# f32 matmuls as pairs of 64-column tiles on TensorE, in a kernel that mixes f32 and bf16 matmuls

## The chip, the cores and the metric

One core of a Trainium2 chip. The time is device microseconds of one execution. Repeated executions of one kernel on one core scatter here: those of the kernel before lie up to 1.3% below and 2.4% above their median. So beside the times this text uses the lengths of stages read from the profiles, which repeat far better. A stage length comes from one profile of each kernel. Each run also has the mean granted clock of TensorE (1.0 is full speed). A run is marked slow when it is more than 1.5% above the fastest of its kernel; on one core that only means the upper part of the scatter.

## The reference

Linear attention on sketched features, then a Fourier mix with a small MLP. Cut to what matters (batch 4, 4 heads, 1088 positions, head size 32, sketch 8):

```python
def phi(x):                                  # 64 features from two projections of 8
    a, b = S1 @ x, S2 @ x                    # per position
    return outer(a, b).reshape(64)
kv  = sum_s phi(k)[s] (x) v[s]               # 64 x 32 per head ("kv sums")
z   = sum_s phi(k)[s]
out = (phi(q) @ kv) / (phi(q) @ z + 1e-6)    # "numerators" and denominators
# then, per batch: real part of the 2-D FFT, residual, normalization, MLP with ReLU
```

## The kernel before

All work is in a fixed order of steps (a timetable of some 1,100), each on one engine: PE (TensorE, the matmuls), DVE (VectorE), ACT (ScalarE) or POOL (GpSimd). The four batches overlap: attention of batch b+1 runs beside the Fourier mix and MLP of batch b. Attention matmuls have f32 operands, those of the mix bf16. Three kinds of f32 matmul concern us; each uses the full 128x128 array:

```python
# k projections: 9 chunks of 128 positions; the moving operand is 64 columns, twice
PE.matmul(_v(bt(bks[c // 4]), 0, 128, 128 * (c % 4), [[1, 128]]),
          kT(s)[:, 128 * c : 128 * c + 128], _v(sblk, 0, 128, 0, [[0, 2], [1, 64]]),
          start=True, stop=True, skip_group_check=True)
# ... cut ...
# kv sums: 9 chunks x 2 pairs of heads; only the two 64x64 diagonal blocks are read later
rhs = _v(vx(s), 0, 128, 32 * c + 1280 * p, [[320, 4], [1, 32]])
PE.matmul(bt(bkv)[:, 128 * p : 128 * p + 128], _v(kp(s, c), 0, n, 128 * p, [[1, 128]]), rhs,
          start=(seen[0] + seen[1] == 0), stop=(seen[p] == 8), skip_group_check=True)
# ... cut: kvz copies of the sums, by ACT and DVE ...
# numerators: 9 chunks x 2 pairs of heads, 66 columns
PE.matmul(bt(bk)[:, o : o + 66], lh, kvz(s, p, i & 1)[:, :], start=True, stop=True,
          skip_group_check=True)
```

The q projections are f32 too, and already run as eight 32x64 tiles at a time. The bf16 matmuls use the full array. In the profile, tile names tell the groups apart: `sblk,kT` are k projections, `vx,kp` kv sums, `kvz,qp` numerators, `tab,fo` and `tab,xb` the first Fourier stage.

## Time and profile before

| | before |
|---|---|
| median of 3 runs | 107.97 us (106.48 to 109.22) |
| span of the profiled run, mean clock | 106.3 us, 0.969 |
| PE, DVE, ACT busy | 84%, 75%, 47% |
| f32 steps as above (all four batches) | 36 + 72 + 72 = 180 |

From the page of the kernel before: the span, the busy strips (40 slices of 2.66 us; tenths), and lines of two f32 groups on PE (matmul) and PEld (weight load). Columns of a group: total busy us, mean ns of one; then idle time before it.

```profile
span 106.3 us, 2601 instructions
...
PE   5985989999799959999977999999996979998000
...
PEclk9999999999999999999999999999999999999755
DMA  2999999999950090000000000203000212223341
...
L591 PE MATMUL bank<-kvz,qp 128*128 128x66 f32 x144 | 21.8, 263 | 1.1 <-ACT kvz L271 1.1
L591 PEld LDWEIGHTS bank<-kvz,qp 128*128 128x128 f32 x144 | 20.6, 191 | 2.8 <-ACT kvz L271 1.3
L504 PE MATMUL bank<-vx,kp 128*128 128x128 f32 x144 | 19.7, 277 | 1.1 <-DMA vx<-in_v_dram 1.1
```

DMA is full until about 30 us; PE is nearly full from there. Each f32 step has two records (x144 for 72 steps): two passes. Records overlap, so a mean of 263 ns is not the cost of one; the starts are. In the timeline of weight loads, two in a row take 0.30 us though one alone takes 0.19: they start 112 ns apart, whether 66 or 128 columns stream. A step costs 222 ns.

The existing tiled matmuls show that a change of tiling is not free. The weight loads of the kernel before, around a block of q projections:

```profile
22.43 0.30 PEld L591 LDWEIGHTS bank<-kvz,qp 128*128 128x128 f32 x2
22.80 0.23 PEld L543 LDWEIGHTS bank<-qT,eb 32*64 32x64 f32 x16
23.84 0.30 PEld L591 LDWEIGHTS bank<-kvz,qp 128*128 128x128 f32 x2 [0.81 <-ACT ab L271]
```

The last full-array matmul before that block started at 22.595 us and the first tiled load at 22.798, 203 ns later, with no wait that the profile shows; without a change of tiling the load behind a full-array matmul starts 1 to 3 ns after it (633 of 737 in this trace). The recorded texts call this extra time a drain.

The chain of waits (start, length):

```profile
38.36 0.19 ACT kvz L271
38.60 0.66 PE bank L591 x4
...
45.00 0.17 PE bank L591 x2
45.17 0.14 PE bank L646
45.33 0.41 ACT zt L271
...
78.60 0.18 DVE den L596
```

**A** is the start of the first numerator after the kvz copies of batch 1 (38.60 us), **B** the end of the twelfth matmul of the first Fourier stage (45.59), **C** the end of the last numerator matmul (78.49), which releases `den`; **D** the end of the span. Up to A the chain is DMA, then POOL and DVE; from A to B it is PE.

### The profile page before, as it was taken

The numbers are of one execution on the slowest core, as the hardware profiler recorded it, in microseconds if no ns is written. First come the engines' busy times: TensorE is split into PE (matmuls) and PEld (weight loads), VectorE is DVE, ScalarE is ACT, GpSimd is POOL, SyncE is SP. The second block draws the span as 40 slices with busy tenths as digits, with TensorE's granted clock in tenths as the row PEclk, the third lists the DMA queues.
The fourth block names the chain that finished last, engine by engine and source line by source line (L and its number), as shares of the span: only waits on it lengthen the run. The fifth ranks groups of instructions, "written<-read, shape, count | busy, mean of one in ns | idle before, by whom it ended". The sixth has DMA issues, their size and how long they took to land.

```text
span 106.3 us, 2601 instructions
## 1 busy us (share of the span) xinstructions
PE 89.4 (84%) x940; PEld 72.3 (68%) x943; DVE 80.2 (75%) x266; ACT 50.4 (47%) x140; POOL 42.0 (39%) x87
## 2 busy tenths in 40 slices
PE   5985989999799959999977999999996979998000
PEld 3672379969399949997743898739895957756000
DVE  1538969685888846999575999789999799998300
ACT  4011520417101030025579757868866979996000
POOL 8813832099119991419300100321939730500000
PEclk9999999999999999999999999999999999999755
DMA  2999999999950090000000000203000212223341
GB/s 77 291 361 268 261 317 250 301 357 188 253 132 10 7 236 11 0 0 0 9 0 0 0 0 24 81 0 99 3 6 0 72 26 70 60 71 82 102 119 48
DMA packets 9620, 11.14 MB, mean 105 GB/s; under 512 B 1032, under 2 KB 8200, under 8 KB 9608
## 3 DMA queue, kind: packets, MB, share of 16 engines
q1 hardware_dynamic: 8920, 10.70, 37.6%
q10 hardware_dynamic: 688, 0.28, 1.0%
q8 instruction: 7, 0.11, 0.5%
q14 instruction: 5, 0.04, 0.1%
HBM read 8.75 MB, written 2.23 MB: 103 GB/s over the span
## 4 chain that ended last, share of the span: by engine, by line
DVE 29%; DMA 24%; PE 15%; ACT 13%; SPq 5%; POOL 3%; issue 2%; DVEq 0%; ACTq 0%; POOLq 0%
DMA vx<-in_v_dram 24%; ACT hT L768 5%; DVE ob L805 5%; DVE fo L632 5%; PE bank L591 5%; DVE st L739 4%; DVE xb L603 4%; ACT us L271 4%; DVE yf L622 3%; PE bank L646 3%; PE bank L504 2%; PE bank L543 2%; SPq L420 2%; SPq L428 2%; POOL kp L488 2%
## 5 line engine op out<-in xcount | busy, mean ns | idle before, releaser
L591 PE MATMUL bank<-kvz,qp 128*128 128x66 f32 x144 | 21.8, 263 | 1.1 <-ACT kvz L271 1.1
L591 PEld LDWEIGHTS bank<-kvz,qp 128*128 128x128 f32 x144 | 20.6, 191 | 2.8 <-ACT kvz L271 1.3
L504 PE MATMUL bank<-vx,kp 128*128 128x128 f32 x144 | 19.7, 277 | 1.1 <-DMA vx<-in_v_dram 1.1
L488 POOL TENSOR_TENSOR kp<-ab 128x256 f32<-128x256 f32 x25 | 15.0, 628 | 13.0 <-ACT ab L271 7.9
L504 PEld LDWEIGHTS bank<-vx,kp 128*128 128x128 f32 x144 | 17.8, 192 | 1.5 <-issue 1.4
L768 ACT ACTIVATE hT<-bank 128x512 bf16<-128x512 f32 x28 | 15.2, 611 | 0.6 <-PE bank L760 0.6
L795 PE MATMUL bank<-w2b,hT 128*128 128x128 bf16 x144 | 12.2, 220 | 0.5 <-ACT hT L768 0.5
L573 DVE TENSOR_TENSOR qp<-bank,bsb 128x512 f32<-128x512 f32 (+1 forms) x24 | 12.2, 542 | 0.1
L271 ACT CAST zt<-bank 128x256 bf16<-128x256 f32 (+1 forms) x21 | 7.3, 403 | 9.5 <-PE bank L646 8.3
L469 PE MATMUL bank<-sblk,kT 128*128 128x128 f32 x72 | 11.2, 281 | 0.6 <-DVE sblk L361 0.6
L739 DVE BATCH_NORM_STATS2 st<-bank 128x6 f32<-128x128 f32 (+1 forms) x36 | 8.9, 279 | 3.7 <-ACT ub L271 2.0
L795 PEld LDWEIGHTS <-hT 128*128 128x128 bf16 x144 | 9.6, 100 | 2.9 <-ACT hT L768 1.3
L469 PEld LDWEIGHTS bank<-sblk,kT 128*128 128x128 f32 x72 | 9.5, 192 | 2.2 <-issue 1.3
L805 DVE SCALAR_TENSOR_TENSOR ob<-bank,rs,us 128x128 f32<-128x128 f32 (+1 forms) x36 | 10.4, 335 | 0.6 <-PE bank L795 0.5
L271 ACT COPY bsb<-bank 128x512 f32<-128x512 f32 (+1 forms) x19 | 8.2, 491 | 5.1 <-PE bank L543 3.2
L760 PE MATMUL bank<-uT,w1c 128*128 128x512 bf16 x29 | 9.8, 378 | 0.6 <-ACT uT L271 0.6
L271 ACT COPY ab<-bank 128x256 f32<-128x256 f32 (+1 forms) x8 | 2.2, 293 | 16.2 <-PE bank L469 16.2
L622 POOL TENSOR_TENSOR yf<-xb 128x512 f32<-128x512 bf16 x5 | 6.2, 1256 | 8.1 <-DVE xb L603 6.4
L632 POOL TENSOR_TENSOR fo<-yf 128x256 bf16<-128x256 f32 x11 | 9.2, 856 | 0.2
L646 PE MATMUL bank<-tab,fo 128*128 128x288 bf16 x32 | 7.8, 287 | 1.7 <-DVE fo L632 1.1
L273 POOL CAST ub<-us 128x512 bf16<-128x512 f32 (+1 forms) x9 | 4.6, 508 | 10.1 <-ACT us L271 8.6
L451 DVE STREAM_TRANSPOSE kT<-kin 128x512 f32<-128x512 f32 x8 | 5.4, 694 | 3.7 <-DMA kin<-in_k_dram 3.7
(77 smaller groups left out, 152.3 us busy)
## 6 DMA issues: line engine op xcount, KB each, us to landing
vx<-in_v_dram SPq DMA_DIRECT2D x16, 160.0 KB
qin<-in_q_dram SPq DMA_DIRECT2D x4, 544.0 KB
out_dram<-ob SPq DMA_DIRECT2D x28, 64.0 KB
kin<-in_k_dram SPq DMA_DIRECT2D x3, 544.0 KB
tab<-tab_d SPq DMA_DIRECT2D x1, 864.0 KB
kin<-in_k_dram SPq DMA_DIRECT2D x1, 288.0 KB
kin<-in_k_dram SPq DMA_DIRECT2D x1, 256.0 KB
w1f<-in_moe_w_ch_dram SPq DMA_DIRECT2D x1, 256.0 KB
```

Source lines behind the costliest of these rows:

```text
L271: SE.copy(o, i)
L469: PE.matmul(_v(bt(bks[c // 4]), 0, 128, 128 * (c % 4), [[1, 128]]), kT(s)[:, 128 * c : 128 * c + 128], _v(sblk, 0, 128, 0, [[0, 2], [1, 64]]),
L488: eng.tensor_tensor(out=_v(kp(s, c), 0, 128, 0, [[64, NH], [8, 8], [1, 8]]), in0=_v(bt(bks[i]) if dv else ab(s, i), 0, 128, (128 if dv els ...
L504: PE.matmul(bt(bkv)[:, 128 * p : 128 * p + 128], _v(kp(s, c), 0, n, 128 * p, [[1, 128]]), rhs, start=(seen[0] + seen[1] == 0), stop=(seen[ ...
L573: P.add(dve(nd, lambda e, p=p, i=i, nd=nd, dd=dd, bA=bA: e.tensor_tensor(out=qp(s, p, i)[:, 0:nd], in0=_v(bt(bA), 0, 128, 0, dd), in1=_v(b ...
L591: PE.matmul(bt(bk)[:, o : o + 66], lh, kvz(s, p, i & 1)[:, :], start=True, stop=True, skip_group_check=True)
L632: eng.tensor_tensor(out=fo(s, n)[:, :, :], in0=yf(s, o)[:, :, 0, :], in1=yf(s, o)[:, :, 1, :], op=opx)
L646: PE.matmul(bt(bk)[:, 0:288], lh, tab[:, kpar, 3 * cs + m, :], start=(m == 0), stop=(m == 2))
L739: P.add(dve(128, lambda e, m=m, nt=nt, i=i, bu=bu: e.bn_stats(_v(st6(s, m), 0, nt, 6 * i, [[1, 6]]), _v(bt(bu), 0, nt, 128 * i, [[1, 128]] ...
L768: SE.activation(out=hT(s, m)[:, c, :], in_=bt(bh)[:, :], func=ACT.Relu)
L795: pe(bfmm(128), lambda m=m, i=i, c=c, bo=bo: PE.matmul(bt(bo)[:, 128 * i : 128 * i + 128], hT(s, m)[:, c, 128 * i : 128 * i + 128] if m < ...
L805: P.add(dve(128, lambda e, m=m, i=i, nt=nt, bo=bo: e.scalar_tensor_tensor(out=_v(ob(s, m), 0, nt, 128 * i, [[1, 128]]), in0=_v(bt(bo), 0, ...
```

## The change

Each f32 step becomes two matmuls side by side, each with 64 of the 128 weight columns, in two 128x64 tiles. The k projections and the kv sums also stream 64 columns in place of 128. The intent is to load weights of both tiles at once and so halve the PE time of f32 steps. The order of steps stays. Core of the diff (cut: lines between the three places, and how the numerators compute their offsets):

```diff
-                PE.matmul(_v(bt(bks[c // 4]), 0, 128, 128 * (c % 4), [[1, 128]]),
-                          kT(s)[:, 128 * c : 128 * c + 128], _v(sblk, 0, 128, 0, [[0, 2], [1, 64]]),
-                          start=True, stop=True, skip_group_check=True)
+                for th in range(2):
+                    PE.matmul(_v(bt(bks[c // 4]), 64 * th, 64, 128 * (c % 4), [[1, 64]]),
+                              kT(s)[:, 128 * c + 64 * th : 128 * c + 64 * th + 64], sblk[:, :],
+                              start=True, stop=True, skip_group_check=True)
 ... cut ...
-                    PE.matmul(bt(bkv)[:, 128 * p : 128 * p + 128],
-                              _v(kp(s, c), 0, n, 128 * p, [[1, 128]]), rhs,
-                              start=(seen[0] + seen[1] == 0), stop=(seen[p] == 8),
-                              skip_group_check=True)
+                    for hh in range(2):
+                        PE.matmul(
+                            _v(bt(bkv), 64 * hh, 64, 128 * p + 64 * hh, [[1, 64]]),
+                            _v(kp(s, c), 0, n, 128 * p + 64 * hh, [[1, 64]]),
+                            _v(vx(s), 0, 128, 32 * c + 1280 * p + 640 * hh, [[320, 2], [1, 32]]),
+                            start=(seen[0] + seen[1] == 0), stop=(seen[p] == 8),
+                            skip_group_check=True)
 ... cut ...
-                        PE.matmul(bt(bk)[:, o : o + 66], lh, kvz(s, p, i & 1)[:, :], start=True,
-                                  stop=True, skip_group_check=True)
+                        for th in range(2):
+                            PE.matmul(_v(bt(bk), 64 * th, 64, 132 * ti + 66 * p, [[1, 66]]),
+                                      qp(s, p, i)[:, o + 64 * th : o + 64 * th + 64],
+                                      kvz(s, p, i & 1)[:, :], start=True, stop=True,
+                                      skip_group_check=True)
```

More of the change, by code (lines that the diff above doesn't have):

```diff
@@ L468, in e @@
             def e(c=c):
-                PE.matmul(_v(bt(bks[c // 4]), 0, 128, 128 * (c % 4), [[1, 128]]),
-                          kT(s)[:, 128 * c : 128 * c + 128], _v(sblk, 0, 128, 0, [[0, 2], [1, 64]]),
-                          start=True, stop=True, skip_group_check=True)
-            pe(f32mm(128), e, [("kT" if c < 8 else "kTr", b), ("kTpad", s), "sblk", "warm"],
+                for th in range(2):
+                    PE.matmul(_v(bt(bks[c // 4]), 64 * th, 64, 128 * (c % 4), [[1, 64]]),
+                              kT(s)[:, 128 * c + 64 * th : 128 * c + 64 * th + 64], sblk[:, :],
+                              start=True, stop=True, skip_group_check=True)
+            pe(f32mm(64, 64), e, [("kT" if c < 8 else "kTr", b), ("kTpad", s), "sblk", "warm"],
                [bks[c // 4]], key=K("pab", c), writes=[("pab", b, c // 4)], t=T + 1 + 0.05 * c)
@@ L502, in e @@
                 def e(c=c, p=p, n=n):
-                    rhs = _v(vx(s), 0, 128, 32 * c + 1280 * p, [[320, 4], [1, 32]])
-                    PE.matmul(bt(bkv)[:, 128 * p : 128 * p + 128],
-                              _v(kp(s, c), 0, n, 128 * p, [[1, 128]]), rhs,
-                              start=(seen[0] + seen[1] == 0), stop=(seen[p] == 8),
-                              skip_group_check=True)
+                    for hh in range(2):
[5 more added lines that the diff above has]
+                            skip_group_check=True)
                     seen[p] += 1
-                pe(f32mm(128), e,
+                pe(f32mm(64, 64), e,
                    [(("kp", c), b), ("vx", b), ("vone", s)] + ([("vr", b)] if c == 8 else []),
@@ L586, in e @@
                             o = 256 * ((0, 1, 1, 0)[x % 4]) + 128 * (x // 4)
-                            lh = qp(s, p, i)[:, o : o + 128]
                         else:
-                            lh = qp(s, p, 2)[:, :]
-                        o = 132 * ti + 66 * p
-                        PE.matmul(bt(bk)[:, o : o + 66], lh, kvz(s, p, i & 1)[:, :], start=True,
-                                  stop=True, skip_group_check=True)
-                    pe(f32mm(66), e, [(("qp", p, i), b), (("kvz", p, i & 1), b)], [bk],
+                            o = 0
+                        for th in range(2):
[3 more added lines that the diff above has]
+                                      skip_group_check=True)
+                    pe(f32mm(66, 64), e, [(("qp", p, i), b), (("kvz", p, i & 1), b)], [bk],
                        key=K("pnd", g), writes=[("pnd", b, g)], t=T + 10 + 2 * g)
```

## The prediction

> **What bounds the kernel now.** Chain of waits: until 32 us the v loads (24% of the span), then POOL and DVE to 38.5 us; TensorE from 38.6 to 45.3 and from 58.3 to 63.3 us. Busy time by stage has PE full from 58 to 78.5 us (20.2 of 20.5 us), DVE close (18.5). The last numerator matmul ends at 78.5 us, den of batch 3 starts at 78.6. After that PE does bf16 alone, and DVE (18.3 of 19.5 us) and ACT bound.
>
> **Cost of one step.** In the timeline an f32 matmul is two passes, each with a weight load of 128 columns; loads start every 112 ns whether 66 or 128 columns stream, so a step costs 222 ns. There are 180 steps (groups: 72 + 144 + 144 records).
>
> **What tiles save.** The q projections already run in 32x64 tiles: eight tiles, pairs of which share rows and differ in columns, load weights within 55 ns of one another and stream together; passes of 64 columns follow every 57 ns. So a step of two 64-column tiles should cost 115 ns, a saving of 107, or 19 us of PE time over all.
>
> **What they cost.** [...] between full-array and tiled matmuls the next weight load starts some 92 ns after the last column has streamed (203 ns after the last f32 record's start, 147 ns after a bf16 one's), not 2 ns after that start; then the load is exposed, 52 ns for 64 columns. Today f32 and bf16 share the full array. After the change every border between them is a switch: I estimate 0.12 to 0.15 us each. The PE records have 95 such borders.
>
> **By stage** (steps, borders; saving, cost at 0.14):
> - before 37.4 us: 96, 3: -10.2, +0.4 us. Nearly all lost: q and v still land at 32 to 33 us, and DVE is full from there to the kvz copies at 37.5. At most 0.4 us earlier.
> - 37.4 to 46: 32, 26: -3.4, +3.6. Nothing.
> - 46 to 58: 12, 7: small; DVE and ACT bound.
> - 58 to 79: 40, 59: -4.3, +8.3. PE is full; f32 steps stand singly between bf16. Of +4.0 us some goes into PE's few stalls, leaving +2 to +4 at the last numerators, which release the rest.
>
> So the change removes PE time where DMA binds, and adds it where PE binds. **Predicted 111.2 us, range 107.6 to 113.8.** Chances: faster by over 2% 0.12, within 2% 0.20, slower by over 2% 0.68.
>
> **What shows it.** Right: in f32 runs before 37 us pairs of tiles overlap, 115 ns a step; the kvz copies stay within 0.5 us; gaps of 150 ns between a bf16 matmul and a lone f32 step; the last numerator matmul ends at 80.5 to 82.5 us; from there the tail keeps its 28 us. DVE and ACT operations keep their durations.
>
> **What would make it wrong.** (1) A switch between 128x64 and 128x128 may drain less than those seen, which also change the row size: then 58 to 79 us loses 4 us of PE work and the kernel gains 2 to 4. (2) Weight loads of two tiles over all 128 rows may not overlap (the trace shows it for 32 rows alone): then nothing is saved and the loss nears 6 us or more. (3) Delays may feed back through DVE and ACT, or more may be absorbed after 79 us, which leaves it within 2%.

## More of the kernel before

PE timeline of the kernel before (start us, length us), in a stage where f32 steps stand between bf16 matmuls:

```profile
43.70 0.29 PE L646 MATMUL bank<-tab,fo 128*128 128x288 bf16 x1
43.82 0.33 PE L591 MATMUL bank<-kvz,qp 128*128 128x66 f32 x2
43.99 0.27 PE L690 MATMUL bank<-xb,cd 128*128 128x256 bf16 x1
44.10 0.34 PE L591 MATMUL bank<-kvz,qp 128*128 128x66 f32 x2
44.27 0.29 PE L646 MATMUL bank<-tab,fo 128*128 128x288 bf16 x1
```

From one bf16 matmul to the next past one f32 step: 0.28 to 0.29 us. Mixing costs nothing here: in the single records of this trace most f32 passes behind a bf16 matmul of 288 columns start 122 to 123 ns after it, as another bf16 matmul does, and the bf16 matmul behind an f32 pass starts 111 to 112 ns after it, as another f32 pass does.

## The result, and the profile after

| | before | after |
|---|---|---|
| median, 4 runs each on one chip | 107.69 us | 116.97 us (116.17 to 117.72) |
| mean clock of the runs after | | 0.878 to 0.910 |

The ratio is 1.090, 95% interval 1.076 to 1.104. A ratio here is the mean time of one kernel's fast runs over that of the other's of the same rounds, so not quite the ratio of the medians. The kernel is 9% slower, where 3% was forecast.

The page after, the same lines:

```profile
span 115.9 us, 3325 instructions
...
PE   5969975994559499999978999999999789999100
...
PEclk9999999599985955556999999999999999999995
DMA  3899999999811700000000000202100030313341
...
L594 PE MATMUL bank<-kvz,qp 128*64 128x66 f32 x288 | 21.2, 258 | 3.0 <-ACT kvz L271 3.0
L594 PEld LDWEIGHTS bank<-kvz,qp 128*64 128x64 f32 x288 | 14.3, 153 | 11.8 <-issue 6.0
...
L506 PE MATMUL bank<-vx,kp 128*64 128x64 f32 x288 | 15.0, 254 | 4.1 <-DMA vx<-in_v_dram 4.0
```

The line that was not foreseen is PEclk (one run was profiled, but the mean clock is low in all four): three dips between slices 8 and 19 (2.9 us each). The trace's clock records give the bounds: half clock from 20.3 to 23.7, from 33.9 to 37.4 and from 40.8 to 54.4 us. Busy time of the kernel after in exactly the windows of the clock (us from the span's start; length; busy us of each engine with its count of instructions; then clock, DMA share, GB/s):

```profile
core 0: us, PE busy (x) PEld busy (x) DVE busy (x) ACT busy (x) POOL busy (x), PEclk, DMA share, GB/s
27.11:30.52 3.41, 1.78 (x58) 1.65 (x55) 3.28 (x7) 0.37 (x1) 0.29 (x1) 1.00 1.10 230
30.52:33.94 3.42, 1.09 (x38) 0.98 (x35) 0.96 (x3) 0.21 (x1) 0.89 (x3) 1.00 0.31 83
33.94:37.35 3.41, 3.41 (x69) 3.37 (x64) 2.75 (x4) 0.39 (x2) 3.41 (x6) 0.50 0.05 10
37.35:40.76 3.41, 1.52 (x25) 0.91 (x26) 2.20 (x6) 0.99 (x6) 3.23 (x6) 1.00 0.71 190
40.76:44.17 3.41, 3.41 (x40) 2.11 (x40) 1.90 (x7) 0.00 (x0) 0.58 (x2) 0.50 0.00 0
...
51.00:54.42 3.42, 3.42 (x46) 2.52 (x53) 2.62 (x8) 0.64 (x2) 0.84 (x1) 0.50 0.00 0
```

The second and third dip each follow a window in which PE worked less than half of the time: 1.09 and 1.52 of 3.4 us (the first likewise: 1.56 us from 16.87 to 20.28). PE, with its early steps twice as fast, waits longer for loads and for the kvz copies. The kernel before has no such window between 11 and 96 us (its next one, 1.67 us from 96.31 us, is followed by half clock in the last 6.6 us); its windows ahead of and across A:

```profile
34.78:38.19 3.41, 2.74 (x25) 2.51 (x23) 2.92 (x7) 0.65 (x5) 3.23 (x5) 1.00 0.29 84
38.19:41.60 3.41, 3.00 (x40) 2.87 (x41) 1.57 (x7) 0.53 (x3) 2.08 (x4) 1.00 0.54 113
```

PE timeline after, at half clock:

```profile
44.99 0.42 PE L651 MATMUL bank<-tab,xb 128*128 128x288 bf16 x1
45.34 0.49 PE L594 MATMUL bank<-kvz,qp 128*64 128x66 f32 x4
45.77 0.42 PE L651 MATMUL bank<-tab,xb 128*128 128x288 bf16 x1
```

and at full clock:

```profile
69.60 0.34 PE L594 MATMUL bank<-kvz,qp 128*64 128x66 f32 x4
69.87 0.28 PE L695 MATMUL bank<-xb,cd 128*128 128x256 bf16 x1
70.09 0.33 PE L594 MATMUL bank<-kvz,qp 128*64 128x66 f32 x3
```

From bf16 start to bf16 start past a lone step: 0.78 us at half clock (44.99 to 45.77; the same pair at full clock takes 0.49 us in all_fill below). At full clock one f32 step starts 0.49 us after the one before it (69.60 to 70.09), with one bf16 matmul between. Before, the like intervals were 0.28 to 0.29 us. In long f32 runs the tiles do what was intended: the trace's single records show a step every 117 ns at about 14 us, both tiles in flight.

The chain after, at the same points:

```profile
39.44 0.19 ACT kvz L271
39.67 0.45 PE bank L594 x8
...
50.73 0.22 PE bank L594 x4
50.95 0.37 PE bank L651
51.34 0.41 ACT zt L271
...
88.12 0.18 DVE den L601
```

| stage (us) | before | after | difference |
|---|---|---|---|
| start to A | 38.60 | 39.67 | +1.07 |
| A to B (half clock in it) | 6.99 (0) | 12.40 (11.3) | +5.41 |
| B to C (half clock in it) | 32.91 (0) | 35.93 (2.3) | +3.02 |
| C to D | 27.83 | 27.91 | +0.08 |

### The profile page after: what moved, and what is told of

It reads as the page before. It is cut to its first block, busy times and chain, and to the rows that moved or that the text cites. A ratio compares the mean times of both kernels' runs of the same rounds, so it can differ in the third digit from the quotient of the medians.

```text
span 115.9 us, 3325 instructions
## 1 busy us (share of the span) xinstructions
PE 94.5 (82%) x1303; PEld 62.9 (54%) x1303; DVE 80.9 (70%) x266; ACT 51.7 (45%) x140; POOL 42.0 (36%) x87
## 4 chain that ended last, share of the span: by engine, by line
PE 33%; DMA 23%; DVE 18%; ACT 10%; SPq 4%; POOL 3%; issue 1%; DVEq 0%; ACTq 0%; POOLq 0%
DMA vx<-in_v_dram 23%; PE bank L594 12%; PE bank L651 5%; ACT hT L773 5%; PE bank L547 4%; DVE fo L637 3%; DVE st L744 3%; PE bank L800 3%; DVE ob L810 3%; PE bank L765 3%; PE bank L506 2%; ACT us L271 2%; DVE yf L627 2%; SPq L420 2%; POOL kp L489 2%; DVE zt L273 2%
## 5 line engine op out<-in xcount | busy, mean ns | idle before, releaser
L594 PE MATMUL bank<-kvz,qp 128*64 128x66 f32 x288 | 21.2, 258 | 3.0 <-ACT kvz L271 3.0
L594 PEld LDWEIGHTS bank<-kvz,qp 128*64 128x64 f32 x288 | 14.3, 153 | 11.8 <-issue 6.0
L506 PE MATMUL bank<-vx,kp 128*64 128x64 f32 x288 | 15.0, 254 | 4.1 <-DMA vx<-in_v_dram 4.0
L773 ACT ACTIVATE hT<-bank 128x512 bf16<-128x512 f32 x28 | 15.9, 606 | 1.1 <-PE bank L765 0.8
L506 PEld LDWEIGHTS bank<-vx,kp 128*64 128x64 f32 x288 | 12.9, 163 | 6.4 <-issue 6.1
L271 ACT CAST zt<-bank 128x256 bf16<-128x256 f32 (+1 forms) x21 | 7.4, 392 | 14.8 <-PE bank L651 13.7
L765 PE MATMUL bank<-uT,w1c 128*128 128x512 bf16 x32 | 10.7, 381 | 0.7 <-ACT uT L271 0.7
L651 PE MATMUL bank<-tab,fo 128*128 128x288 bf16 x32 | 8.6, 314 | 2.2 <-POOL fo L637 0.8
L470 PE MATMUL bank<-sblk,kT 128*64 128x64 f32 x144 | 9.3, 257 | 0.2 <-DVE sblk L361 0.2
L470 PEld LDWEIGHTS bank<-sblk,kT 128*64 128x64 f32 x144 | 7.5, 168 | 2.7 <-issue 1.8
L462 DVE STREAM_TRANSPOSE qT<-qin 128x576 f32<-128x576 f32 (+1 forms) x8 | 5.5, 724 | 4.0 <-DMA qin<-in_q_dram 4.0
```

Of the source, the lines that this page charges most:

```text
L271: SE.copy(o, i)
L470: PE.matmul(_v(bt(bks[c // 4]), 64 * th, 64, 128 * (c % 4), [[1, 64]]), kT(s)[:, 128 * c + 64 * th : 128 * c + 64 * th + 64], sblk[:, :], ...
L506: PE.matmul(_v(bt(bkv), 64 * hh, 64, 128 * p + 64 * hh, [[1, 64]]), _v(kp(s, c), 0, n, 128 * p + 64 * hh, [[1, 64]]), _v(vx(s), 0, 128, 32 ...
L594: PE.matmul(_v(bt(bk), 64 * th, 64, 132 * ti + 66 * p, [[1, 66]]), qp(s, p, i)[:, o + 64 * th : o + 64 * th + 64], kvz(s, p, i & 1)[:, :], ...
L651: PE.matmul(bt(bk)[:, 0:288], lh, tab[:, kpar, 3 * cs + m, :], start=(m == 0), stop=(m == 2))
L765: pe(bfmm(512), lambda m=m, c=c, bh=bh: PE.matmul(bt(bh)[:, :], w1c[:, 128 * c : 128 * c + 128], uT(s, m)[:, :], start=True, stop=True), [ ...
```

## The experiments

Theory A, formed on this result: there are two separate costs. Changes of tiling cost PE time wherever f32 and bf16 alternate, as forecast; and the time that the tiles save early becomes idle PE time, after which the clock falls to half and stays there in a stage that is bound by PE. Theory B: the borders alone do it; they are dearer than forecast, and the waits at them lower the clock.

A switch, put into all three kinds of step, picks which of the 180 steps, counted in PE order, are tiled. The first 96 lie before A in the kernel before.

```diff
+    f32_step = [0]
+    def in_tiles(kind):
+        f32_step[0] += 1
+        return f32_step[0] <= 96        # "early"; "late": > 96; "mid": 97 to 128; "tail": > 140
```

In `full_grouped` it returns False. All kernels gave correct results.

### early and late: one half of the change each

> Tiles only in the first 96 f32 steps in PE order (those that the profile before has ahead of 37.4 us); the other 84 in the full array, so hardly any border is a switch. Theory A (two costs: borders from 58 to 79 us, some 3.5 us, and a TensorE clock that falls to half because PE, done sooner with its early steps, idles on the loads, some 5 us): the clock still falls in windows ahead of 41 us, and where one of them reaches into 38.6 to 46 us the time is 1 to 4 us over before, 108.5 to 112 us; without the borders it recovers a window sooner than in the changed kernel. Theory B (the borders alone: drains are dearer than estimated, and the drains themselves lower the clock): same as before within 1%, and clock 1.0 from 38 us on.

> The reverse: the first 96 f32 steps in the full array as before, the last 84 in tiles, so all borders from 37.4 us on are switches. Theory A: the clock stays 1.0 up to 95 us; the last numerator ends 3 to 4.5 us later than before; time 111 to 112.5 us. Theory B: the clock falls in 38 to 54 us as in the changed kernel, time 115 to 118 us.

Measured on one chip: before 108.37 us (median of 7), early 111.3 (110.13 to 112.85), late 113.89 (111.39 to 114.61). Most runs of these two count as slow beside their own fastest, so I give medians and no interval, and rest on the stages. In the profile, early has half clock from 20.4 to 23.8, off the chain, and from 37.4 to 44.3 us; A to B takes 9.52 us, and everything after B is as before (B to C 32.92). The windows of early, the first of them idle, then two at half clock:

```profile
33.96:37.37 3.41, 1.08 (x38) 0.95 (x33) 2.93 (x6) 0.18 (x1) 3.41 (x5) 1.00 0.40 105
37.37:40.80 3.43, 2.42 (x13) 2.01 (x13) 1.25 (x4) 0.99 (x6) 2.86 (x5) 0.51 0.38 91
40.80:44.20 3.40, 3.40 (x32) 3.28 (x32) 1.90 (x7) 0.00 (x0) 0.00 (x0) 0.50 0.00 0
```

There is no tiled f32 step from A on in this kernel, so theory B can't explain its 2.5 us. Late has the clock at 1.0 from A to B, which takes 8.16 us: 1.17 more than before and 4.24 less than in the full change. B to C is 36.50 us, with one half-clock window (56.0 to 59.4). The clock was not full throughout as theory A expected, and the median is above its range. The two halves together (+2.9 and +5.5 us of medians) make up nearly the whole loss.

### early_twice: more work, to hold the clock

```diff
-                for th in range(2):
+                for th in [0, 1] * times(2):       # 2 for the first 96 steps, else 1
```

(likewise in the kv sums, into unused columns, and in the numerators)

> The changed kernel with each of its first 96 f32 steps made twice (the second into columns that nobody reads, or the same result again), so that an early step costs what it did before, 230 ns, in tiles. More work, all in the stage bound by loads. Theory A: the clock no longer falls ahead of 54 us and the kernel is about 5 us faster than the changed one, 111 to 113 us. Theory B: no faster than the changed kernel, 116.5 to 119 us.

Measured: 117.36 us, ratio 1.081 to before; no faster than the change. By the time, theory A's expectation missed. The profile says why it is no test of it: from A to B the clock was full and the stage took 8.16 us, as theory A has it, but A itself came at 42.18 us. From 18.65 us PE stood for 2.94 us, waiting for nothing that the profile shows; a 16 KB packet of the instruction queue ran among the loads from 19.1 to 20.3 us of that time; and the clock was half from 22.7 to 26.1 us. What held PE for the 2.94 us is not shown.

### early_fill, all_fill: idle work of few instructions

Steps 61 to 96 alone get idle work, as bf16 matmuls of zeros into columns that nobody reads (and k projections made twice):

```diff
+                    if 60 < f32_step[0] <= 96 and c < 8:
+                        for hh in range(2):
+                            PE.matmul(_v(bt(bkv), 64 * hh, 64, 256, [[1, 256]]), dumw[:, 0:64],
+                                      dumw[:, 0:256], start=False, stop=True, skip_group_check=True)
```

> The kernel with tiles in the first 96 f32 steps alone, plus idle work for PE in steps 61 to 96: each kv-sum step but the last of a batch is followed by a pair of bf16 matmuls of zeros, 256 columns in the same two tiles, into columns that nobody reads, and each k projection is made twice. Theory A (PE that is done early lets the clock fall, and the low clock costs the 3 us of that kernel): no window of half clock from 37 to 46 us, time back to that of before within 1%, 107 to 109 us. Rival (the clock falls for another reason[...]): half clock there as before the filling, 110 to 112 us.

> The changed kernel (all 180 steps in tiles) with the same idle work in steps 61 to 96. Theory A: the half clock of 41 to 54 us is gone or shortened to one window, the stage from 38.6 us to the last bf16 matmul of the first Fourier stage takes about 9 us instead of 13.8, and the time falls from 117 to 111.5 to 114.5 us, that of tiles in the late steps alone. Rival (drains by themselves lower the clock there): 116 to 118 us.

On one chip, before 109.03 us (7 runs). early_fill: 109.44 us (107.26 to 110.24). The half-clock time from A to B shrank from 5.5 to 3.4 us and the stage from 9.52 to 8.63, so part of the way: the expectation of no such window missed. (The stages of 13.8 us in this expectation and of 8.4 and 10.9 us in the next ones count from the first bf16 matmul of the Fourier stage, 1.4 us ahead of A in the profiles that they speak of.) all_fill: 113.47 us against 116.97 for the change; ratio to its before 1.037, interval 1.023 to 1.052. Its clock was full from A to C: A to B 8.16 us, B to C 36.20. Its windows ahead of and across A (columns as above), and PE at the pair that took 0.78 us at half clock:

```profile
37.53:40.94 3.41, 3.12 (x88) 2.70 (x83) 2.85 (x6) 1.18 (x7) 3.23 (x5) 1.00 0.40 105
40.94:44.36 3.42, 3.42 (x60) 2.30 (x58) 1.80 (x7) 0.00 (x0) 1.24 (x3) 1.00 0.45 92
...
44.23 0.30 PE L678 MATMUL bank<-tab,xb 128*128 128x288 bf16 x1
44.45 0.34 PE L621 MATMUL bank<-kvz,qp 128*64 128x66 f32 x4
44.72 0.30 PE L678 MATMUL bank<-tab,xb 128*128 128x288 bf16 x1
```

The tiles are the same as in the change, all the borders are there, and 4.24 us of the loss from A to B are gone. That is the clock's share, and theory B is out for this stage: with PE busy for 3.12 of the 3.41 us ahead of it, the waits at the borders did not lower the clock (1.00 in both windows).

### early_fill2 and early_fill3: the last idle microsecond

> The filled kernel with tiles in the first 96 steps, with one more piece of idle work: nine bf16 matmuls of zeros, 224 columns, full array, after the first bf16 matmul of the first Fourier stage, where PE otherwise waits about 1 us for the kvz copies. In the first filling one half-clock window from 41 us was left, and its four runs went by their mean clock: 107.3 us at 0.974, 109.0 to 110.2 us at 0.94. Theory A: most runs now have a mean clock of 0.96 or more (the window at 20 us remains in some) and take 106.5 to 108.5 us, within 1% of before; runs with a lower clock stand 2 to 3 us higher. Rival (the idle time is not what lowers the clock): mean clock 0.94 in most runs and 109 to 111 us.

> In the second filling the nine matmuls of zeros stood in the wrong place: they went with a bf16 step that PE reaches at 45.3 us, on the chain, and cost about 0.9 us there, while PE still idled from 37.4 to 38.5 us. Here they follow the bf16 step that PE reaches first, ahead of that idle time. Theory A: no half clock from 37 to 46 us in the profile, 38.5 us to the last matmul of the first Fourier stage back at 8.4 us from 10.9, and the time within 1% of before, 106.5 to 108.5 us, in most runs. Rival: half clock there as before, 109 to 111 us.

early_fill2 missed: the nine matmuls came at 45.4 us, on the chain, and took 0.86 us there; 110.06 us (6 runs; before 107.17, ratio 1.024, interval 1.017 to 1.032), with half clock from 40.5 to 43.9 us as in the first filling. Three of its runs had a clock of 0.976 to 0.984 and yet took 109.1 to 110.7 us, so the mean clock of a run does not tell its time. early_fill3 puts them right behind the first bf16 matmul that PE reaches:

```diff
+                        f32_step.append(n)
+                        for _ in range(9 if len(f32_step) == 2 else 0):
+                            PE.matmul(bt(bk)[:, 288:512], dumw[:, 0:128], dumw[:, 0:224],
+                                      start=False, stop=True, skip_group_check=True)
```

Busy time in early_fill3, same columns:

```profile
36.20:39.60 3.40, 3.40 (x97) 3.23 (x94) 3.17 (x7) 0.76 (x5) 3.23 (x5) 1.00 0.23 64
39.60:43.00 3.40, 3.40 (x47) 3.26 (x46) 1.46 (x7) 0.41 (x3) 1.67 (x3) 1.00 0.56 134
```

No idle time, no half clock, and A to B takes 6.90 us (before: 6.99; the same tiles unfilled: 9.52). The median is 109.20 us against 108.61 (ratio of the fast runs 1.003, interval 0.987 to 1.019); it lies above the range of 106.5 to 108.5 that I had written when before stood at 107.2. In this one profile A came 1.5 us later, with half clock from 29.3 to 32.8 us. So matmuls of zeros, in time that PE would idle, take away the clock's whole cost in that stage, and the kernel shows no gain over before.

### mid and tail: the borders by stage

> Tiles in f32 steps 97 to 128 alone, those that before has from 37.4 to 46 us: 32 steps, 26 borders. The prediction took this stage for neutral (-3.4 and +3.6 us) with the clock up. If a border costs 0.14 us and the clock stays up: 107.5 to 109.5 us, within 1.5% of before. If the drains of this stage by themselves lower the clock: half clock from about 41 us on, 111 to 114 us.

> Tiles in the last 40 f32 steps alone (58 to 79 us in before): 40 steps, 59 borders, lone steps between bf16 matmuls. The term of the prediction by itself, without early idle time: the last numerator ends 2 to 4 us later than before, clock 1.0 from 5 us on; 110.5 to 112.5 us. If instead the late loss came with the low clock of earlier stages: within 1% of before.

On one chip, before 107.39 us (11 runs). mid: 110.33 us (6 runs, 107.83 to 113.87; above the expected 107.5 to 109.5, and too scattered for a verdict). Its profile has the clock full and A to B at 8.16 us, so theory B's half clock is not there; but the run of 113.87 us had a mean clock of 0.910 where the others had 0.972 to 0.984. In that run it may have fallen without early tiles; no trace of it exists, and this stays open. tail: 110.98 us, ratio 1.037 (1.031 to 1.042); A to B 6.99 as before, B to C 36.41, that is +3.50 us at full clock (one half-clock window, at 11.2 us, lies far ahead of A). This is the forecast term by itself, inside its range of 2 to 4 us.

### late_grouped, full_grouped, tail_grouped: fewer borders, same instructions

Each step of the given range is moved up on PE behind the f32 step before it, past at most 8 (tail: 2) bf16 matmuls, as far as its inputs and its bank allow.

```diff
     steps = P.order(TIMETABLE)
+    steps = gathered(steps, 96, 180, 8)      # tail_grouped: 140, 180, 2
```

> Tiles in the last 84 f32 steps alone, and on PE each of these steps moved up behind the f32 step before it, past at most 8 bf16 matmuls where what it needs allows: 31 borders in place of 97. If the borders are the cost in the late stages: 66 borders fewer at 0.14 us are 9 us of PE time, so PE has about 5 us less work there than in the kernel before; DVE then binds; time 104.5 to 109 us. If the number of PE instructions or the tiles themselves are the cost: 111.5 to 114.5 us as without the grouping.

> The kernel before (no tiles) with the same grouping of the last 84 steps: what the order alone does. Without tiles a border costs nothing, so I expect it within 1.5% of before, 106.5 to 110 us; the gain of the grouped tiles is counted against this one.

> The same 40 steps in tiles, each moved up on PE behind the f32 step before it past at most 2 bf16 matmuls, so that about 24 borders are left of 59; the order before that is untouched. By the numbers of the study: 40 steps save 4.3 us, 24 borders cost 3.4 us, so PE is 0.9 us lighter than before, and DVE is nearly full in this stage: 106.5 to 109 us, at least 2 us faster than the same tiles without grouping. It is also the candidate for a version faster than before; I expect at most 1%.

| | borders in the trace | time | A to B | B to C |
|---|---|---|---|---|
| late (tiles) | 95 | 113.89 us | 8.16 | 36.50 |
| late_grouped (tiles) | 31 | 111.16 | 9.19 | 33.48 |
| full_grouped (no tiles) | 31 | 114.51 | 12.47 | 34.78 |
| tail (tiles) | 95 (59 after 56 us) | 110.98 | 6.99 | 36.41 |
| tail_grouped (tiles) | 69 (33 after 56 us) | 108.93 | 6.99 | 33.20 |

(Before beside late: 108.37; beside the two grouped: 109.03; beside the tails: 107.39. late and late_grouped have one half-clock window between B and C.) My expectation for full_grouped missed, and with it that for late_grouped (104.5 to 109 us): the order alone costs 5% (ratio 1.054, interval 1.043 to 1.066), because f32 steps pulled ahead delay the bf16 matmuls of the first Fourier stage (one run of them holds the chain for 2.51 us, from 47.42 us). In this same order the tiles save 3.3 us, where in the old order they cost 5.5. And with the order before B untouched, 26 borders fewer (35 were expected) make B to C 3.21 us shorter with the same tiles and the same number of matmuls, so neither the count of instructions nor the tiles are the cost, but the borders; only what this one order does without tiles was not run. tail_grouped is 1.2% slower than before (interval 1.002 to 1.021): the candidate for a faster kernel is none, and I found none.

## Why the prediction was wrong

- **Costs per step: right.** 117 ns per tiled step in dense runs (forecast 115), both tiles in flight. Condition (2) of the prediction, loads that don't overlap over 128 rows, did not occur: the loads of the two tiles, 136 ns long each, start 7 ns apart (69.013 and 69.020 us), beside the records of matmuls over the same rows (from 68.960 us, 272 ns long).
- **Borders: right in kind, a little low in one stage.** Condition (1), a cheaper change between 128x64 and 128x128, did not occur: at full clock the bf16 load after a lone step starts 150 ns after the start of its last 66-column pass (single records: 69.075 and 69.225 us), which by estimate leaves about 0.1 us after the last column (150 less 66 x 0.83 is 95 ns, at the 0.83 ns a column that is worked out below). Around the q projections it is 92 ns: the next full-array load starts 516 ns after the start of a last tiled pass of 512 columns and 145 ns after one of 64. Behind a full-array f32 pass the next tiled load starts 203 to 204 ns after its start, whether 66 or 128 columns streamed. Between B and C the forecast was +2 to +4 us; tail shows +3.50 alone, the full change +3.02. From A to B the forecast said "37.4 to 46: 32, 26: -3.4, +3.6. Nothing"; at full clock it is +1.17 us in mid, late, early_twice and all_fill alike. That stage holds, counted in the trace, 24 steps and 24 borders, so a border there costs (1.17 + 24 x 0.105) / 24 = 0.15 us, the top of the estimate. In tail from B to C it is (3.50 + 40 x 0.105) / 59 = 0.13 us.
- **The step that failed:** "before 37.4 us ... Nearly all lost", followed by "Nothing" for 37.4 to 46 us. I took a saving where DMA binds for worth nothing and costing nothing. It made PE idle, 2.3 us (one gap) and 1.9 us (gaps of 0.79 and 1.10) of two windows of 3.41 us (from 30.5 and from 37.4 us), and the clock fell to half after each, the second time for 13.7 us from 40.8 us on, in the one stage before 58 us where PE is on the chain. That term is 12.40 - 8.16 = 4.24 us. early shows it without any tile in that stage (+2.53), all_fill and early_fill3 take it away by matmuls of zeros.
- **The low clock lasted longer with borders.** early left the half clock after 2 windows, the full change after 4, though PE had a record in flight all the time. The traces let me estimate what such records hide: the share of a window in which PE streams columns, tiles that stream together counted once. For a column I take 0.42 ns in bf16 (in before, back-to-back matmuls of 128 and 512 columns start 55 and 215 ns apart) and 0.83 ns in an f32 pass ((516 - 145) / 448 from the loads above), and twice that at half clock (behind a group of q projections of 512 columns the next group starts 434 ns after the last start at full clock, at 22.846 us in before, and 867 ns after it at half clock, at 21.218 us in after). By this estimate the four windows of the full change at half clock have 0.70, 0.69, 0.70 and 0.82, and the clock came back after the last; the second one of early, with no border in it, has 0.86, and the clock came back after it. So the borders did not bring the clock down here (all_fill streams 0.59 of the windows from 40.9 and 44.4 us, and stays full). Whether they kept it down, as the lower shares of the first three windows suggest, is not shown: no run was made to test it.
- **Start to A, +1.07 us:** not the change. In before, early, late, mid, tail, tail_grouped and after, A follows POOL's copy behind the third v load by 6.70 to 6.72 us; that copy starts at 31.66 us in mid, at 32.97 after and at 32.70 in tail, which has no tile before 58 us. So it is the scatter of load arrival.
- **After C:** right, 27.91 us against 27.83.

The sum: +1.07 (loads), +1.17 and +3.02 (borders, less what the tiles save), +4.24 (clock), +0.08 make the 9.6 us between the two spans. Without the clock's term the time would be 116.97 - 4.24 = 112.7 us (all_fill measured 113.5), inside the forecast range.

In the traces of before and after every clock record but the last lasts 3.41 us or a whole multiple of it, at 1.0 or at 0.5. The prediction did not ask what the clock would do.

## What to carry to other kernels

Before speeding up PE work that waits for something else, ask what PE will do with the time: here half clock followed windows with 2.3 and 1.9 of 3.41 us idle, and the saving off the chain became a loss of 4.24 us on it; look at the clock strip first. Tiles of another shape pay in runs: here a tiled step saves 0.11 us and each border with full-array matmuls costs 0.13 to 0.15 us, so by these numbers fewer than about three steps per run lose (two borders are 0.26 to 0.30 us). To judge such a change, measure stages between fixed points of the profile; for the same tiles at full clock A to B repeats to 0.1 us here (6.90 to 6.99, and 8.16 us), where whole runs scatter by 2% and more.
